# State's read in two runs one down sooner, values ahead of the last down, keys times values behind it

## The chip, the cores and the metric

The kernel runs on one core of a Trainium2 chip. The metric is the device time of one execution in microseconds; lower is better. A core has five engines with queues of their own: TensorE (PE in the profile, with its weight loads apart as PEld), VectorE (DVE), ScalarE (ACT), GpSimd (POOL) and SyncE (SP), which here only issues DMAs. Each engine works its queue off in order, and engines wait for one another through semaphores.

## The reference

A gated linear attention with a state per batch and head, and then an MLP whose activation is a SoLU with a layer norm:

```python
# q, k, v, alpha: batch 4, heads 8, seq 768, head_dim 48
for t in range(S):
    state = alpha[:, :, t, :, None] * state + np.einsum('bhd,bhe->bhde', k[:, :, t], v[:, :, t])
    y[:, :, t] = np.einsum('bhd,bhde->bhe', q[:, :, t], state)

x = y.transpose(0, 2, 1, 3).reshape(B * S, H * D)      # 3072 tokens x 384
h = x @ w_in                                           # 384 -> 1024
e = np.exp(h - h_max)
solu = h * (e / (np.sum(e, axis=-1, keepdims=True) + 1e-09))
ln = (solu - mu) / np.sqrt(var + 1e-06) * g_ln
return ln @ w_out                                      # 1024 -> 384
```

Everything is float32.

## The kernel before

**Tiles.** The sequence is cut into six groups of 128 tokens; a group holds these tokens for all four batches, 512 columns. Inside a group the attention is a masked product (scores of keys and queries, both scaled by products of alpha, times the values), and what came before the group enters through the state, which is read once per group and then renewed. The MLP of a group runs in eight steps s (0 to 7), one for each 128 of the 1024 hidden features.

**The pieces that the change and the prediction name:**

- `up(g, s)` (L382 to L407): three matmuls (w_in times x, each shown as two records) make the 512 columns of h for one step; ACT takes the exponential e (L404), DVE forms u = h*e (L405), ACT squares it (L406). h has two PSUM banks, so an up waits until the product of the up two before it has been made.
- `running` (L409): the sums of e (on POOL) and of u squared (on DVE) over the steps, into p (L421). `token_sums` (L448) turns p into sums per token by small matmuls ("rows", L456).
- `down(n, half)` (L495): for one batch of a group, eight matmuls of 385 columns against w_out, in two halves of four (L501). A group's downs are done during the next group, one half behind each up. `finish(n)` (L506): four short DVE instructions, a power on POOL (r, L532), the scaling on ACT (o_sb, L534), and the store.
- `alpha_T`, `scan_back`, `scan_on` (L187, L206, L211): transposes and scans on DVE that make the decay products. `alpha_over` (L192): two passes on ACT over the alphas as loaded, which look for values out of range; the next load of alpha may only start behind them, since it overwrites `an`.
- `keys_T`, `keys` (L222, L226): key transposes on DVE and their products with the decay on POOL.
- `scores(g, half)` (L274): 64 small matmuls (32 rows by 128) into four PSUM banks a0 to a3. `masked(half)` (L288): four DVE products that empty these banks into sT (L291).
- `read_state(half)` (L344): 32 small matmuls of q with the state into four PSUM banks y0 to y3, the same four banks as a0 to a3. `read_values` (L352): 64 small matmuls of sT with the values onto the same sums, and then four ACT copies (L359) that put them into x, the input of the next group's up.
- `next_state(g)` (L361): 64 small matmuls of keys times values, "kv", into banks a0 and a1 (so they need two of the x copies), and two additions into the state on DVE (L377). The load of v for the next group (`load_v`, L173) overwrites what kv reads.

Each of these matmuls has two records for the product and two for its weight load.

**Order.** The schedule is written by hand: the program order in Python is each engine's order. Groups 0 and 1's attention and group 0's MLP are a prologue written out (up to L811). From then on a loop runs over the groups' MLP (g = 1 to 5) and their eight steps; the attention of group g+1 is woven in by two tables, `first` for g = 1 and `usual` for the later ones. Each step does, in this order: what the table's `head` names, the up, a `finish` if one is due, at step 0 the token sums of the group before, `behind`, `running`, `middle`, one half down, `tail`. There are no downs in g = 1, since group 0's are all done in the prologue.

```python
    usual = dict(
        head={4: "keys_back", 5: "masked0", 6: "masked1"},
        behind={0: "v keys", 1: "on2 on0 on1", 2: "lasts firsts", 3: "apart", 5: "decay", 6: "alpha", 7: "back"},
        tail={4: "scores0", 5: "scores1", 6: "begin read0", 7: "values"},
        middle={7: "read1"},
    )
```

So PE's order around the end of a usual group is: up 6, half down, read0, up 7, read1, half down, values, kv, up 0 of the next group, rows.

Of the kernel before, what the change touches and what calls it, by code (L numbers as in the profile page):

```python
# [32 lines left out]
def fast_path(ctx, tc, q, k, v, alpha, moe_w_in, moe_w_out, moe_g_ln, out):  # L33
# [23 lines left out]
    HF = FC // 2  # L57
# [37 lines left out]
    over = const.tile([P, G, 2], FP, name="over")  # L95
# [35 lines left out]
    def load(src, dst, g):  # L131
        t = slice(g * P, (g + 1) * P)
        for b in range(B):
            nc.sync.dma_start(
                out=dst[32 * b : 32 * b + 32].rearrange("t h u d -> t h (u d)"),
                in_=src[b, :, t, :].rearrange("h (t u) d -> t h (u d)", u=TQ),
            )
# [40 lines left out]
    def firsts(src, dst):  # L178
        nc.vector.transpose(out=dst.rearrange("p h (t u) -> p h u t", u=TQ), in_=src[:, :, :, 0:E0])  # L179

    def lasts(src, dst):
        nc.vector.transpose(
            out=dst.rearrange("p j (i t u) -> p u j i t", u=TQ, i=2),
            in_=src[:, :, :, E0:D].rearrange("p (j i) u d -> p u j i d", i=2),
        )

    def alpha_T(g):  # L187
        nc.gpsimd.memset(aT[:, :, 0:1], 0.0)
        firsts(an, aT[:, 0:H, 1:SW])
        lasts(an, aT[:, H:NB, 1:SW])  # L190

    def alpha_over(g):  # L192
        x = an.rearrange("p h u d -> p (h u d)")
        sq = one.tile([P, 768], FP, name="sq").bitcast(U8)[:, 0 : x.shape[1]]
        for i, sign in enumerate((1.0, -1.0)):
            nc.scalar.activation(  # L196
                out=sq, in_=x, func=AF.Relu, scale=sign, bias=mone, accum_out=over[:, g, i : i + 1]
            )
# [12 lines left out]
    def scan_on(g, i):  # L211
        part = slice(NP * i, NP * i + NP)
        s = seed[i % 2]
        if i == 2:
            nc.vector.tensor_copy(out=fend[:, g], in_=h4[:, :, 1])

        least = small.tile([P, NP, 1], FP, name="least")
        nc.vector.tensor_scalar(out=least, in0=h4[:, part, 1:2], scalar1=LEAST, scalar2=None, op0=ALU.max)  # L218
        nc.vector.reciprocal(out=s[:, :, 0:1], in_=least)
        scan(aT[:, part], aT[:, part], s, False)  # L220
# [50 lines left out]
    def banks(name, shape, n=B):  # L271
        return [ps_a.tile([P] + shape, FP, tag=f"a{b}", name=f"{name}{b}") for b in range(n)]
# [71 lines left out]
    def read_state(half):  # L344
        for four in range(8 * half, 8 * half + 8, 4):
            for c in range(2):
                for n, h, e in parts[four : four + 4]:
                    for i in range(2):
                        p = slice(64 * i, 64 * i + 64)
                        y_mm(2 * i + c, n, 64 * i, state[p, c, e(h)], q64[p, c, h, 0:P])  # L350

    def read_values(g, batches=range(B)):  # L352
        if 0 in batches:
            gr[g]["x"] = pair.tile([P, KC, B, P], FP, name="x")
        for b in batches:
            for m, (n, h, e) in enumerate(parts):
                y_mm(b, n, 0, vn[:, b, e(h)], sT[:, b, h], m >= len(parts) - 4)
        for b in batches:
            nc.scalar.copy(out=gr[g]["x"][:, :, b], in_=reading["y"][b])  # L359

    def next_state(g):  # L361
        kv = banks("kv", [H, D], 2)
        for h in range(H):
            for c in range(2):
                for r in range(4):
                    b = 2 * (r // 2) + c
                    nc.tensor.matmul(
                        kv[c][quarter(r), h], lhsT=kg[:, b, h, E0 * (r % 2) : E0 * (r % 2) + E0],
                        rhs=vn[:, b, HW * h + E1 : HW * h + HW], start=True, stop=True,
                        tile_position=(0, 32 * r), skip_group_check=True,  # L370
                    )
        for c in range(2):
            s = held(state, c)
            if g == 0:
                nc.scalar.copy(out=s, in_=kv[c])
            else:
                nc.vector.tensor_tensor(out=s, in0=s, in1=kv[c], op=ALU.add)  # L377
# [114 lines left out]
        d["r"] = small.tile([P, B], FP, name="r4")  # L492
        nc.gpsimd.tensor_tensor(out=d["r"], in0=s[:, :, 3], in1=mhalf.to_broadcast([P, B]), op=ALU.pow)

    def down(n, half):  # L495
        g, b = divmod(n, B)
        d = st[n]
        if half == 0:
            d["o"] = ps_o.tile([P, 512], FP, tag="o", name="o")
        for f in range(half * HF, half * HF + HF):  # L500
            nc.tensor.matmul(  # L501
                d["o"][:, 0 : DM + 1], lhsT=u_of(g, f)[:, b * P : b * P + P], rhs=w_out[:, f], start=(f == 0),
                stop=(f == FC - 1), skip_group_check=True,
            )
# [178 lines left out]
    for i in range(3):  # L683
        part = slice(NP * i, NP * i + NP)
# [4 lines left out]
    for i in (2, 0, 1):  # L689
        if i == 1:  # L690
            scan_on(0, i)
        part = slice(NP * i, NP * i + NP)
# [66 lines left out]
    for i in range(3):  # L759
        scan_back(1, i)  # L760
        part = slice(NP * i, NP * i + NP)
# [18 lines left out]
    for i in range(2):  # L780
        scan_on(1, i)
        part = slice(NP * i, NP * i + NP)
# [12 lines left out]
    down(3, 0)  # L795
    read_begin()
    read_state(0)
    down(3, 1)
    read_state(1)
    alpha_over(2)  # L800
    load(alpha, an, 3)
    for i in range(3):
        scan_back(2, i)
    keys_T(2)
    keys(2)
    load(k, kn, 3)
    scan_on(2, 2)
    scan_on(2, 0)
    read_values(1)
    next_state(1)  # L810
    finish(3)  # L811

    usual = dict(
        head={4: "keys_back", 5: "masked0", 6: "masked1"},
        behind={0: "v keys", 1: "on2 on0 on1", 2: "lasts firsts", 3: "apart", 5: "decay", 6: "alpha", 7: "back"},
        tail={4: "scores0", 5: "scores1", 6: "begin read0", 7: "values"},
        middle={7: "read1"},
    )  # L820
    first = dict(
        head={3: "keys_back", 5: "masked0", 6: "masked1"},
        behind={0: "v", 1: "on1", 2: "lasts firsts", 3: "apart", 5: "decay", 7: "alpha back"},
        tail={4: "scores0", 5: "scores1", 6: "begin read0", 7: "values"},
        middle={7: "read1"},
    )

    def attend(a, what):

        more = a + 1 < G  # L830
        if what == "v":
            load_v(a)
        elif what == "keys":
            keys_T(a)
            keys(a)
            if more:
                load(k, kn, a + 1)
        elif what[:2] == "on":
            scan_on(a, int(what[2]))
        elif what == "lasts":  # L840
            lasts(qn, qe[:, :, 0:P])
            ends_of_decay()
            queries(2)
            move_lasts()
        elif what == "firsts":
            firsts(qn, qv[:, 0:H, 0:P])
            queries(0)
            queries(1)
            move_firsts()
            if more:  # L850
                load(q, qn, a + 1)
        elif what == "apart":
            apart()
        elif what == "decay":
            decay(a)
        elif what == "keys_back":
            if more:
                keys_back(a)
        elif what[:6] == "scores":
            scores(a, int(what[6]))  # L860
        elif what[:6] == "masked":
            masked(int(what[6]))
        elif what == "alpha" and more:
            alpha_T(a + 1)
            alpha_over(a + 1)
            if a + 2 < G:
                load(alpha, an, a + 2)
        elif what == "back" and more:
            for i in range(3):
                scan_back(a + 1, i)  # L870
        elif what == "begin":
            read_begin()
        elif what[:4] == "read":
            read_state(int(what[4]))
        elif what == "values":
            read_values(a)
            if more:
                next_state(a)

    centres = {4: (0, 1), 6: (2, 3), 7: (4, 5, 6, 7)}  # L880
    todo = []
    for g in range(1, G + 1):
        rise, att = g < G, g + 1 < G
        plan = first if g == 1 else usual

        def at(where, s):
            for what in plan[where].get(s, "").split() if att else ():
                attend(g + 1, what)

        after = None  # L890
        if not rise:
            break
        for s in range(FC):
            at("head", s)
            if rise:
                up(g, s)
            if after is not None:
                finish(after)
                after = None
            if s == 0 and g > 1:  # L900
                token_sums(g - 1)
            at("behind", s)
            for f in centres.get(s, ()) if g == 1 else ():
                centre(f)
            if rise and s:
                running(g, s)
            at("middle", s)
            if todo:
                n, half = todo.pop(0)
                down(n, half)  # L910
                if half:
                    after = n
            at("tail", s)
        if after is not None:
            finish(after)
        todo = [(n, half) for n in range(g * B, g * B + B) for half in range(2)]
# [493 lines left out]
```

## Time and profile before

| | us |
|---|---|
| median of 3 runs | 387.33 (387.31 to 387.72) |
| the profiled execution, whole | 388.88 |
| its span, first to last instruction | 387.1 |
| DVE's mask products `sT<-a,mask` (L291), mean of one | 0.683 |
| ACT's x copies `x<-y` (L359), mean of one | 0.480 |
| kv matmuls (L367), median of one record | 0.206 |

The profile shows one execution. Times in its lists are microseconds from the span's start. A line of the timeline gives start, length, engine, source line, operation, what it writes and reads, the shapes, how many instructions were merged into the line, and in brackets how long the engine was idle before it and what ended that. "issue" there means that the trace shows nothing that the engine waited for. A line of the waits gives the waiting instruction, the one that released it, the total, how many times, and the longest. Matmuls overlap in their pipeline, so what a run of them costs is read from the start of one run to the start of the next rather than from the lengths.

### The profile page before, as it was taken

The page shows a single profiled execution, that of the slowest core. Times are in us where ns is not written, and L with a number is a line of the kernel's source. Part 1 is how long each engine was busy: PE and PEld are TensorE (multiplying, and loading weights), DVE is VectorE, ACT ScalarE, POOL GpSimd, SP SyncE. Part 2 cuts the span into 40 slices and gives each one's busy share as a digit, 9 for nine tenths or more (in the row PEclk, how much of TensorE's full clock was granted, in tenths as well). Part 3 has the DMA queues.
Part 4 walks back from the last instruction along what each step waited for, and adds up shares of the span by engine and source line. Part 5 has one row for each costly group of instructions (what it writes and reads, how often), then busy time and mean ns, then how long its engine had stood idle before and what let it go on. Part 6 is the DMA issues. An engine that isn't in the chain of part 4 may idle for free. (4 is left out here: it accounts for less than half of the span.)

```text
span 387.1 us, 10060 instructions
## 1 busy us (share of the span) xinstructions
PE 365.6 (94%) x4341; PEld 219.3 (57%) x4341; DVE 250.7 (65%) x413; ACT 144.5 (37%) x255; POOL 111.5 (29%) x122
## 2 busy tenths in 40 slices
PE   8798899988979998999999999998999999999994
PEld 8685335656645556555557555665556565555652
DVE  0989878996997858885584875664875413444600
ACT  2628566681415426134253153342142132222100
POOL 6000000000232992437130466210475211323200
PEclk9989999999989999999999999999999999999999
DMA  9891978248355535717142627003123000000011
GB/s 182 166 323 51 221 220 200 47 97 183 92 131 104 116 79 102 147 35 161 37 105 47 140 62 172 13 11 70 36 63 89 22 16 8 23 21 20 22 44 47
DMA packets 72439, 36.05 MB, mean 93 GB/s; under 512 B 48185, under 2 KB 69953, under 8 KB 72385
## 3 DMA queue, kind: packets, MB, share of 16 engines
q1 hardware_dynamic: 71360, 34.39, 37.6%
q10 hardware_dynamic: 1024, 0.92, 0.7%
q8 instruction: 36, 0.59, 0.7%
q14 instruction: 19, 0.15, 0.1%
HBM read 25.30 MB, written 4.72 MB: 78 GB/s over the span
## 5 line engine op out<-in xcount | busy, mean ns | idle before, releaser
L390 PE MATMUL h<-x,w_in 128*128 128x512 f32 x288 | 134.8, 608 | 3.4 <-DVE room L405 1.6
L501 PE MATMUL o<-w_out,room 128*128 128x385 f32 x384 | 133.1, 491 | 1.1 <-DVE least L218 1.1
L501 PEld LDWEIGHTS o<-w_out,room 128*128 128x128 f32 x384 | 71.6, 190 | 56.8 <-issue 15.3
L390 PEld LDWEIGHTS h<-x,w_in 128*128 128x128 f32 x288 | 53.1, 192 | 63.5 <-issue 49.2
L405 DVE TENSOR_TENSOR room<-h,e 128x512 f32<-128x512 f32 x40 | 27.7, 693 | 62.6 <-ACT e L404 62.6
L404 ACT ACTIVATE e<-h 128x512 f32<-128x512 f32 x40 | 23.9, 597 | 89.1 <-PE h L390 88.5
L421 POOL TENSOR_TENSOR p<-p,e 128x512 f32<-128x512 f32 x30 | 40.8, 1360 | 21.9 <-ACT e L404 21.5
L406 ACT ACTIVATE u<-room 128x512 f32<-128x512 f32 x40 | 25.2, 630 | 42.5 <-DVE room L405 42.5
L532 POOL TENSOR_TENSOR r<-sums,mhalf 128x1 f32<-128x1 f32 x20 | 12.5, 626 | 91.5 <-DVE sums L524 91.5
L291 DVE TENSOR_TENSOR sT<-a,mask 128x512 f32<-128x512 f32 x44 | 27.3, 683 | 15.3 <-PE a L280 15.3
L280 PE MATMUL a<-qv,kT 32*128 32x128 f32 x704 | 26.2, 289 | 3.9 <-DVE least L218 2.0
L280 PEld LDWEIGHTS a<-qv,kT 32*128 32x128 f32 x704 | 23.2, 196 | 11.0 <-issue 2.3
L421 DVE TENSOR_TENSOR p<-p,u 128x512 f32<-128x512 f32 x30 | 23.6, 786 | 8.4 <-ACT u L406 8.4
L204 DVE TENSOR_TENSOR_SCAN hT<-aT,unit 128x516 f32<-128x516 f32 x18 | 22.3, 1285 | 8.7 <-ACT aT L677 8.6
L204 DVE TENSOR_TENSOR_SCAN aT<-aT,seed 128x516 f32<-128x516 f32 x18 | 25.0, 1391 | 0.6
L329 PE MATMUL y<-sT,vn 128*32 128x128 f32 x768 | 22.6, 273 | 0.4 <-DVE sT L291 0.4
L329 PEld LDWEIGHTS y<-sT,vn 128*32 128x32 f32 x768 | 20.7, 110 | 2.9 <-issue 2.0
L228 POOL TENSOR_TENSOR kT<-kT,hT 128x1024 f32<-128x1024 f32 (+1 forms) x8 | 13.3, 1682 | 29.8 <-DVE kT L179 29.8
L359 ACT COPY x<-y 128x384 f32<-128x384 f32 x24 | 11.2, 480 | 22.7 <-PE y L329 22.7
L196 ACT ACTIVATE sq<-an,mone 128x1536 uint8<-128x1536 f32 x12 | 18.9, 1572 | 0.2
L243 POOL COPY qe<-hT 128x4 f32<-128x4 f32 x5 | 1.0, 191 | 59.4 <-DVE hT L204 59.4
L534 ACT ACTIVATE o_sb<-o,r 128x384 f32<-128x384 f32 x16 | 9.3, 581 | 17.2 <-POOL r L532 17.2
(142 smaller groups left out, 370.2 us busy)
## 6 DMA issues: line engine op xcount, KB each, us to landing
vn<-in_v_dram SPq DMA_DIRECT2D x24, 192.0 KB, 4.5
an<-in_alpha_dram SPq DMA_DIRECT2D x20, 192.0 KB, 4.1
out_dram<-o_sb SPq DMA_DIRECT2D x20, 192.0 KB, 2.0
room<-in_moe_w_in_dram SPq DMA_DIRECT2D x6, 512.0 KB, 7.5
room<-in_moe_w_out_dram SPq DMA_DIRECT2D x8, 384.0 KB, 4.3
kn<-in_k_dram SPq DMA_DIRECT2D x16, 192.0 KB, 3.9
qn<-in_q_dram SPq DMA_DIRECT2D x16, 192.0 KB, 4.7
lot<-qe SPq DMA_DIRECT2D x40, 64.5 KB, 2.1
```

Source lines behind the costliest of these rows:

```text
L196: nc.scalar.activation(out=sq, in_=x, func=AF.Relu, scale=sign, bias=mone, accum_out=over[:, g, i : i + 1])
L204: nc.vector.tensor_tensor_scan(out=o, data0=a, data1=s, initial=1.0, op0=ALU.mult, op1=ALU.add)
L228: nc.gpsimd.tensor_tensor(out=kT[:, part], in0=kT[:, part], in1=hk[:, part], op=ALU.mult)
L280: nc.tensor.matmul(a[b][:, i], lhsT=kT[quarter(b), kb], rhs=qv[quarter(b), qb, 0:P], start=kb == h, stop=kb != h, tile_position=(32 * b, 0 ...
L291: nc.vector.tensor_tensor(out=sT[:, b, half * NP : half * NP + NP], in0=a[b], in1=mask[:, None, :].to_broadcast([P, NP, P]), op=ALU.mult,)
L329: nc.tensor.matmul(y_bank(b)[quarter(r), a], lhsT=lhsT, rhs=rhs, start=(b, r) not in begun, stop=stop, tile_position=(row, 32 * r), skip_g ...
L390: nc.tensor.matmul(h, lhsT=w_in[:, a, f * P : (f + 1) * P], rhs=d["x"][:, a].rearrange("p b t -> p (b t)"), start=(a == 0), stop=(a == KC ...
L404: nc.scalar.activation(out=e, in_=h, func=AF.Exp)
L405: nc.vector.tensor_tensor(out=u, in0=h, in1=e, op=ALU.mult)
L406: nc.scalar.activation(out=u2, in_=u, func=AF.Square)
L421: eng.tensor_tensor(out=p, in0=d[0][i] if f == 1 else p, in1=d[f][i], op=ALU.add)
L501: nc.tensor.matmul(d["o"][:, 0 : DM + 1], lhsT=u_of(g, f)[:, b * P : b * P + P], rhs=w_out[:, f], start=(f == 0), stop=(f == FC - 1), skip ...
```

## The change

In the table for the usual groups the first half of the state's read moves from behind the down of step 6 to ahead of it, the second from ahead of the down of step 7 to behind that of step 6; the values move ahead of the down of step 7, and kv stays behind it, now as an item of its own. In the table for g = 1 the values stand in the middle of step 7, ahead of `alpha_over`, and kv moves behind the first up of the next group. In the prologue, the second half of down(3) is split in two, one part ahead of the read's second half, one behind the values; the values go ahead of `alpha_over`, `finish(3)` ahead of two scans, and kv behind the first up of the loop.

```diff
-    def down(n, half):
+    def down(n, half, part=range(HF)):
         g, b = divmod(n, B)
         d = st[n]
-        if half == 0:
+        if half == 0 and 0 in part:
             d["o"] = ps_o.tile([P, 512], FP, tag="o", name="o")
-        for f in range(half * HF, half * HF + HF):
+        for f in (half * HF + i for i in part):
...
     read_state(0)
-    down(3, 1)
+    down(3, 1, (0, 1))
     read_state(1)
+    read_values(1)
     alpha_over(2)
     load(alpha, an, 3)
     for i in range(3):
...
     keys_T(2)
     keys(2)
     load(k, kn, 3)
+    down(3, 1, (2, 3))
+    finish(3)
     scan_on(2, 2)
     scan_on(2, 0)
-    read_values(1)
-    next_state(1)
-    finish(3)
...
     usual = dict(
         head={4: "keys_back", 5: "masked0", 6: "masked1"},
         behind={0: "v keys", 1: "on2 on0 on1", 2: "lasts firsts", 3: "apart", 5: "decay", 6: "alpha", 7: "back"},
-        tail={4: "scores0", 5: "scores1", 6: "begin read0", 7: "values"},
-        middle={7: "read1"},
+        middle={6: "begin read0", 7: "values"},
+        tail={4: "scores0", 5: "scores1", 6: "read1", 7: "kv"},
     )
     first = dict(
...
-        tail={4: "scores0", 5: "scores1", 6: "begin read0", 7: "values"},
-        middle={7: "read1"},
+        middle={7: "read1 values over"},
+        tail={4: "scores0", 5: "scores1", 6: "begin read0"},
     )
...
         elif what == "alpha" and more:
             alpha_T(a + 1)
+            if a > 2:
+                attend(a, "over")
+        elif what == "over" and more:
             alpha_over(a + 1)
...
         elif what == "values":
             read_values(a)
-            if more:
-                next_state(a)
+        elif what == "kv" and more:
+            next_state(a)
...
             if after is not None:
                 finish(after)
                 after = None
+            if s == 0 and g < 3:
+                next_state(g)
             if s == 0 and g > 1:
                 token_sums(g - 1)
```

## The prediction

> **What bounds the kernel now.** I read the page's busy shares first, then TensorE's (PE's) own waits, then the timeline of PE around the places that the change moves, then the clock there, last VectorE (DVE) and ScalarE (ACT) in the same stretches.
>
> ```profile
> span 387.1 us, 10060 instructions
> PE 365.6 (94%) x4341; PEld 219.3 (57%) x4341; DVE 250.7 (65%) x413; ACT 144.5 (37%) x255; POOL 111.5 (29%) x122
> ...
> PE kv L367 <- issue: 3.7, 2, 2.5
> ...
> PE kv L367 <- ACT x L359: 1.0, 1, 1.0
> PE h L390 <- ACT x L359: 0.6, 1, 0.6
> ```
> PE is the bound: 94% busy. Of its few waits, these three lines (5.3 us of idle time) all lie where the change works: at keys times values (kv) and at the up projection (h) behind the read.
>
> ```profile
> 104.18 3.70 PE L329 MATMUL y<-sT,vn 128*32 128x128 f32 x128
> 107.70 1.46 PE L367 MATMUL kv<-vn,kg 128*32 128x48 f32 x120
> 111.65 0.29 PE L367 MATMUL kv<-vn,kg 128*32 128x48 f32 x8 [2.49 <-issue]
> 111.87 9.69 PE L390 MATMUL h<-x,w_in 128*128 128x512 f32 x18
> ...
> 144.82 3.70 PE L329 MATMUL y<-sT,vn 128*32 128x128 f32 x128
> 149.57 1.86 PE L367 MATMUL kv<-vn,kg 128*32 128x48 f32 x128 [1.04 <-ACT x L359]
> 151.36 2.84 PE L390 MATMUL h<-x,w_in 128*128 128x512 f32 x6
> ...
> 201.96 3.70 PE L329 MATMUL y<-sT,vn 128*32 128x128 f32 x128
> 205.47 1.54 PE L367 MATMUL kv<-vn,kg 128*32 128x48 f32 x128
> ...
> 263.84 0.36 PE L367 MATMUL kv<-vn,kg 128*32 128x48 f32 x10 [1.23 <-issue]
> ...
> 317.71 2.84 PE L390 MATMUL h<-x,w_in 128*128 128x512 f32 x6 [0.60 <-ACT x L359]
> ```
> Five joints between two groups. The first and the fourth stop inside kv for no partner that the profile knows ("issue"), the second waits for ACT's copies of x, the third runs through, the fifth has no kv and waits for x.
>
> ```profile
> 112.32:115.74 3.42, 3.42 (x5) 1.35 (x4) 3.28 (x10) 0.00 (x0) 0.00 (x0) 0.50 0.51 126
> ...
> 113.17 1.23 DVE L204 TENSOR_TENSOR_SCAN aT<-aT,seed 128x516 f32<-128x516 f32 x1
> 114.32 0.99 DVE L377 TENSOR_TENSOR state<-state,kv 128x384 f32<-128x384 f32 x2
> ...
> 117.56 0.69 DVE L405 TENSOR_TENSOR room<-h,e 128x512 f32<-128x512 f32 x1 [1.26 <-ACT e L404]
> ```
> The windows view's last columns are granted clock, DMA share, GB/s: after the stop of 2.49 us PE had half its clock for 3.42 us. And DVE's first up product starts at 117.56 only; up(1,2), the third up projection, needs the bank that it frees (its weights load at 118.39).
>
> [...] DMA queue 8 carries 36 packets of 16,384 bytes, and counted over PE's records the two "issue" stops stand at records 3265 and 7105, 3840 = 15 x 256 apart. [...] the fetch records before the stops begin at 108.79 and 261.63 and end 1.50 and 1.28 us before PE goes on. From entering one block to running the next took 4.26 us at the first stop (DMA share 0.77 at its start) and 3.01 us at the fourth joint; 256 kv instructions alone run in 1.48 us. So a block nearly all kv starves PE. [...] (a 1.23 us scan took 1.88 beside POOL's kT products).
>
> **The change part by part.**
>
> Prices from PE's start-to-start times in group 2: up 2.57 and down 2.59 between full-array work, read half 1.09, values 3.51, kv 1.48; each border between full-array and small-tile matmuls adds 0.10 (up 2.77 and down 2.79 with small work at both sides). From the start of values to an up that only waits for x: 317.71 - 313.41 = 4.30.
>
> *Prologue.* The second half of down(3) is split around read1 and values; the x copies go ahead of alpha_over on ACT (3.5 us there), finish(3) ahead of two scans on DVE, kv behind up(1,0). PE: read0 from 99.02 to 100.30; two downs 1.5; read1 to 102.9; values to 106.4; two downs 1.4 to 107.9; x is ready at 102.9 + 4.3 = 107.2, so up(1,0) needs no wait; to 110.7; kv to 112.2; up(1,1) to 114.9. Kv now shares its block with four matmuls of down and a whole up: 0.1 + 1.4 + 2.8 + 1.3 = 5.6 us against 4.26, so the stop of 2.49 goes and with it the half clock. One block becomes tighter, that from read0 to late in read1, 3.8 us: its successor landed at 101.72, usable at some 103.1 against 102.8. Up to 0.4 us, inside the slack that follows.
>
> What is late next is DVE. It ends the key transposes at 109.31 as before, then runs finish(3) (before 115.23 to 116.30, 1.07 us). POOL's key products hold until 111.77, and the first scan could not end before 112.87 anyway; finish fits in that shadow if it isn't itself locked out (scans end at 114.4 as now), otherwise all shifts by at most 1.07. I take half, 114.9. Then comes the first up product at once: its exp is ready (POOL's r behind the key products to 112.35, o_sb 113.0, exp 113.6), where it started at 117.56 before, because state adds and finish stood ahead of it. So up(1,2) gains 2.65 us: bounds 2.15 (all locked) and 3.5 (PE's own 114.9 against 118.4). The state adds, 0.99, fit in the 1.40 us that DVE idles between two up products. Group 1 passes this on whole: its scores wait for the DVE-POOL-ACT chain, which starts with that product. **-2.65.**
>
> *Group 1 to 2.* alpha_over (1.58 x 2 + 0.19 x 2 = 3.5 us on ACT) no longer stands ahead of the x copies. Up starts 4.30 after values, at 149.12; up 2.77, kv 1.49: the token sums ("rows") start at 153.38 instead of 154.13. Their DVE input ends at 152.21 now, before that by the same shift. The exp of this up waits some 0.5 us for alpha_over, behind a PE with two full matmul runs ahead. **-0.75.**
>
> *Groups 2 to 4.* Read0 goes ahead of down in step 6, read1 behind it, values ahead of the last down, kv behind. Small runs are read0, read1, values, kv, rows where they were read0, read1, values+kv, rows: one more, two borders, **+0.2** in groups 2 and 3 each, none in group 4. Down (2.79) and kv hide the x copies as kv did. Group 3's stop goes: its joint took 264.12 - 257.63 = 6.49 against group 2's 4.99; after, its block holds one down and 233 kv, 4.2 us against 3.01. **-1.50.** Group 2's blocks come out at 5.8 and 4.28 us, the latter as now (4.23) without a stop. Group 4 has down between values and up: 4.30 - 3.51, **-0.8.**
>
> The new wait is read0 for the banks that masked1 frees. Group 2: scores end at 188.84, up ends at 191.5, the four mask products run 188.93 to 191.41. No slack, no loss: banks 1 and 3 are needed 0.3 us after 0 and 2, so 0 to 0.1 a group. Behind the waiting read0 stands only PE's own down, with it all of PE.
>
> *Queues.* SP and POOL keep their order. The alpha loads go out 7 and 3.5 us later (needed a group later), key loads behind them; the loads of v wait for kv, at 112.2 in the prologue and some 2 us later at group 1's end, wanted over 30 us on. The w_out centring on POOL gets a wait on the late downs, over 25 us old by then.
>
> **Sum:** -2.65 - 0.75 + 0.2 - 1.5 + 0.2 - 0.8 = -5.3 us. Profiled execution: span 387.1 to 381.8, with the 1.78 around it 388.88 to 383.6. The median of the runs lies 1.55 below the profiled execution: 387.33 - 5.3 = **382.0**.
>
> **Rivals.**
> - *PE paces the prologue.* If finish(3) hides in POOL's shadow and group 1's chain is no limit: 3.5 instead of 2.65, **381.2** or a little less. Against it: group 1's scores already wait for ACT and DVE.
> - *The prologue gives nothing*, since DVE, with the same work, sets group 1's pace and the product's head start is lost to POOL or transfers: the rest, -2.65, gives **384.7**. For it: DVE is at 7 to 9 tenths there.
> - *The fetch waits move rather than go.* Then only the x waits are gained: -0.75 - 0.8 + 0.4, **386.2**. Against: every block that holds kv gets a full-array run.
> - *Read0 waits for the masks (slower).* Place: step 6 of groups 2, 3, 4, where down covered them. Bounded by that down, 2.79 a group, 8.4 in all: **390.4**. It decides from 1.8 us a group on, i.e. if the masks take nearly double; they took 2.48 in each group, and DVE was idle 1.8 us ahead of them.
>
> **How the numbers follow.** Forecast (381.4 to 382.8) 0.55; PE paces 0.12; prologue gives nothing 0.15; fetch waits move 0.10; slower 0.06; no change 0.02. Some 0.2% (0.8 us) is what a measurement of this kernel can tell from no change: faster 0.91, same 0.03, slower 0.06. The range reaches from a little under the PE-paced case to a little over that without the prologue, 380.6 to 384.9; the moved fetch and the slower case stay outside.
>
> **What would show it.** Right: no "issue" stop inside kv at any joint; clock 1.00 from 100 us on; up(1,2) near 115.7; values followed by down without a wait for x; read0 starting within 0.1 us of up's end. Wrong: a stop of over 1 us at another record a multiple of 256 from 3265; half clock after 110 us; scores of group 1 starting as late as 129; or idle time before read0 put down to DVE's masks.

## The result, and the profile after

| | before | after |
|---|---|---|
| median | 387.52 us (387.31 to 389.16, 4 runs) | 382.58 us (382.24 to 383.32, 4 runs) |
| the profiled execution, whole | 388.88 | 382.77 |
| its span | 387.1 | 381.0 |

The ratio is 0.9863, 95% interval 0.9833 to 0.9894: 4.9 us by the medians. The spans differ by more, 6.1 us, and 1.2 us of that isn't the change's. The windows view of the two profiles at 20 us shows why; its last three columns are granted clock, DMA share and GB/s. First before, then after:

```profile
20.16:23.57 3.41, 3.41 (x75) 3.41 (x71) 2.24 (x3) 0.15 (x1) 0.12 (x1) 0.50 0.96 369
```

```profile
20.10:23.50 3.40, 3.22 (x111) 2.97 (x104) 3.37 (x6) 0.00 (x0) 0.12 (x1) 1.00 1.05 395
```

The profiled execution of before had half its TensorE clock for 3.41 us in the prologue, in code that both kernels share. Read0 (the first half of the state's read), the first instruction near the change, starts at 99.02 before and at 97.78 after, 1.24 us apart. The changed kernel was profiled a second time (in the last run of the experiments below): that time it had the half clock there itself, and its read0 started at 98.94. So all comparisons of profiles below count from read0.

PE's own waits after the change, longest first:

```profile
PE h L390 <- DVE room L405: 2.7, 4, 0.9
PE a L280 <- DVE least L218: 1.8, 1, 1.8
PE a L280 <- DVE qv L783: 1.2, 1, 1.2
PE o L501 <- DVE least L218: 1.1, 1, 1.1
...
PE h L390 <- ACT x L359: 0.6, 1, 0.6
```

The "issue" wait at kv and the waits for x at kv and in group 4 are gone. On top stands a wait of h for DVE's up product, and one wait for x is left. PE's timeline at the joints that the prediction showed:

```profile
101.89 3.80 PE L329 MATMUL y<-sT,vn 128*32 128x128 f32 x128
105.63 1.56 PE L501 MATMUL o<-w_out,room 128*128 128x385 f32 x4
107.03 2.74 PE L390 MATMUL h<-x,w_in 128*128 128x512 f32 x6
109.69 1.57 PE L367 MATMUL kv<-vn,kg 128*32 128x48 f32 x128
111.19 2.84 PE L390 MATMUL h<-x,w_in 128*128 128x512 f32 x6
114.83 2.84 PE L390 MATMUL h<-x,w_in 128*128 128x512 f32 x6 [0.80 <-DVE room L405]
...
145.48 2.84 PE L390 MATMUL h<-x,w_in 128*128 128x512 f32 x6 [0.61 <-ACT x L359]
148.25 1.57 PE L367 MATMUL kv<-vn,kg 128*32 128x48 f32 x128
...
257.19 1.57 PE L367 MATMUL kv<-vn,kg 128*32 128x48 f32 x128
```

Every kv now runs through without a bracket. The first joint has its new wait at the third up (0.80 us for DVE), the second keeps 0.61 us of wait for x ahead of the up.

The time falls into stretches, each from the start of one run of PE instructions to the start of another, so that nothing depends on modelled ends. All are differences to before, in microseconds, from the timelines: A is read0 to the key transposes of group 1 (22.37 before), B from there to the second half of the scores (12.36), C to group 1's token sums (20.38), D, E and F on to those of groups 2, 3 and 4 (55.59, 57.18, 53.59). What follows F took the same within 0.2 everywhere.

| | A | B | C | D | E | F | sum |
|---|---|---|---|---|---|---|---|
| the change | -2.63 | +0.21 | -0.83 | +0.32 | -1.26 | -0.68 | -4.87 |
| the change, profiled again | -2.84 | +0.24 | -0.83 | +0.32 | -1.26 | -0.68 | -5.05 |

So two profiles of one kernel agree within 0.21 us in A and 0.03 us elsewhere, and the sum fits the medians. Five of the profiles below have the change's prologue unaltered; they give -2.73 to -2.95 in A, so -2.63 is the least of seven.

### The profile page after: what moved, and what is told of

Its sections match the earlier page's. It is cut to its first block, busy times and chain, and to the rows that moved or that the text cites. A ratio compares the mean times of both kernels' runs of the same rounds, so it can differ in the third digit from the quotient of the medians.

```text
span 381.0 us, 10060 instructions
## 1 busy us (share of the span) xinstructions
PE 363.3 (95%) x4341; PEld 215.7 (57%) x4341; DVE 251.2 (66%) x413; ACT 144.3 (38%) x255; POOL 112.1 (29%) x122
## 5 line engine op out<-in xcount | busy, mean ns | idle before, releaser
L390 PE MATMUL h<-x,w_in 128*128 128x512 f32 x288 | 133.4, 601 | 3.9 <-DVE room L405 2.7
L280 PE MATMUL a<-qv,kT 32*128 32x128 f32 x704 | 24.9, 278 | 3.9 <-DVE least L218 1.8
L280 PEld LDWEIGHTS a<-qv,kT 32*128 32x128 f32 x704 | 22.0, 186 | 10.9 <-POOL p L421 2.2
```

What stands on the lines that cost most here:

```text
L280: nc.tensor.matmul(a[b][:, i], lhsT=kT[quarter(b), kb], rhs=qv[quarter(b), qb, 0:P], start=kb == h, stop=kb != h, tile_position=(32 * b, 0 ...
L390: nc.tensor.matmul(h, lhsT=w_in[:, a, f * P : (f + 1) * P], rhs=d["x"][:, a].rearrange("p b t -> p (b t)"), start=(a == 0), stop=(a == KC ...
```

## The experiments

### Each part alone

*The prologue's part* (tables as before, kv of the first joint behind the up):

```diff
-    down(3, 1)
+    down(3, 1, (0, 1))
     read_state(1)
+    read_values(1)
     alpha_over(2)
...
+    down(3, 1, (2, 3))
+    finish(3)
     scan_on(2, 2)
     scan_on(2, 0)
-    read_values(1)
-    next_state(1)
-    finish(3)
...
+            if s == 0 and g == 1:
+                next_state(g)
```

> Only the prologue's part of the change (down split, values ahead of the alpha check, finish ahead of two scans, kv of group 0 to 1 behind the first up); the tables stay as before. Theory (steps add up, DVE paces the prologue): the stop inside kv at the first joint and the half clock after it are gone, the third up of group 1 starts 2.3 to 2.7 us sooner, nothing else changes: -2.4 us, ratio 0.994. Rival (the 2.49 us stop and the half clock, 1.7 us, are worth their full length on PE): -4 us. Rival (parts need each other): under 1 us.

*The usual table alone*; the values of group 1 and the prologue stay:

```diff
     usual = dict(
...
-        tail={4: "scores0", 5: "scores1", 6: "begin read0", 7: "values"},
-        middle={7: "read1"},
+        middle={6: "begin read0", 7: "values"},
+        tail={4: "scores0", 5: "scores1", 6: "read1", 7: "kv"},
```

> Only the table of the usual groups changes (read halves one down sooner, values ahead of the last down, kv behind it). Theory: group 2 +0.3 us (one more small run), group 3 -1.26 (the fetch stop inside kv gone), group 4 -0.67: -1.6 us, ratio 0.996. The stop of 2.49 us in the prologue stays. Rival (fetch stops move rather than go): a new stop in groups 2 to 4, no gain beyond 0.7 us.

*The table of group 1 alone:*

```diff
     first = dict(
...
-        tail={4: "scores0", 5: "scores1", 6: "begin read0", 7: "values"},
-        middle={7: "read1"},
+        middle={7: "read1 values over"},
+        tail={4: "scores0", 5: "scores1", 6: "begin read0"},
...
+            if s == 0 and g == 2:
+                next_state(g)
```

> Only the table of group 1 changes (values ahead of the alpha check, kv behind the next up). Theory: token sums of group 1 start 0.75 to 0.85 us sooner, all else as before: -0.8 us, ratio 0.998; the stops in the prologue and in group 3 stay. Rival (the x copies are late for another reason than the alpha check): no change.

Measured, beside a before of 387.1 us:

| | median | ratio | A | B | C | D | E | F |
|---|---|---|---|---|---|---|---|---|
| prologue | 384.86 | 0.9926 (0.9900 to 0.9951) | -2.73 | +0.23 | +0.01 | +0.08 | -0.23 | +0.09 |
| usual table | 386.30 | 0.9976 (0.9962 to 0.9989) | -0.67 | +0.25 | +0.01 | +0.33 | -1.26 | -0.67 |
| group 1's table | 386.28 | 0.9969 (0.9952 to 0.9986) | -0.20 | 0.00 | -0.84 | 0.00 | -0.19 | +0.09 |

In its own stretches each part gains what the whole change gains there, and the three ratios add up to -1.3%, where the change has -1.4%. The parts don't need each other, and the rival that the first stop and the half clock count at full length, 4 us, is out: the prologue's part gives 2.5 us in A and B. Of the small shares elsewhere, the -0.67 in A for the usual table is taken up below; the -0.23 and -0.19 in E are in part a shorter stop of group 3 (1.09 and 1.13 us instead of 1.23), and 0.09 of them comes back in F. The usual table's median gains 0.8 us only, where its stretches D to F give 1.60 and 1.6 was forecast; its interval reaches to 1.5 us. Its executions ranged from 385.36 to 387.70, and what the rest is isn't shown.

That run of the usual table shows more. Its PE timeline in the prologue, where its program is that of before:

```profile
106.16 1.46 PE L367 MATMUL kv<-vn,kg 128*32 128x48 f32 x120
109.70 0.29 PE L367 MATMUL kv<-vn,kg 128*32 128x48 f32 x8 [2.08 <-issue]
109.92 5.42 PE L390 MATMUL h<-x,w_in 128*128 128x512 f32 x12
116.70 2.84 PE L390 MATMUL h<-x,w_in 128*128 128x512 f32 x6 [1.36 <-DVE room L405]
```

A stop again, 0.41 us shorter, but no half clock behind it this time: two ups take 5.42 us. Yet A and B together are only 0.42 us shorter (-0.67 and +0.25), since PE now waits 1.36 us for DVE ahead of the third up. So before, the stop and the half clock stood almost wholly behind DVE: in DVE's timeline of before, which the prediction shows, the state additions start at 114.32 right behind a scan and without a wait, 2.4 us after the end of kv (111.65 + 0.29).

### Are the stops the arrival of instructions?

The kernel before, with 72 more PE records ahead of everything:

```diff
-            nc.tensor.matmul(t[:, 0:P], lhsT=ones, rhs=ones, start=True, stop=True)
+            nc.tensor.matmul(t[:, 0:HW], lhsT=ones, rhs=ones[:, 0:HW], start=True, stop=True)
...
-    warm(18)
+    warm(36)
```

> The kernel before with 36 warm-up matmuls of 64 columns instead of 18 of 128: 18 more matmuls, 72 more PE records ahead of everything else, the same PE work in columns. Theory (stops are the arrival of instruction blocks of 256): every stop comes 72 records earlier in the program. First joint: the stop stands after some 84 of the 128 kv records instead of 120, about 2.0 us. Group 3's joint: after some 82 instead of 118, about 0.8 us. Group 2's joint, which had none, gets one after some 112 kv records, about 1.3 us, since its block now holds 31 records of values and 225 of kv. Group 1's gets none. Time about 0.4 us over before. Rival (the stops are a wait that belongs to the last kv matmuls, such as a PSUM bank or a transfer): they stay after 120 and 118, and group 2 stays free.

PE's timeline at the first joint and at group 2's:

```profile
118.52 1.10 PE L367 MATMUL kv<-vn,kg 128*32 128x48 f32 x84
121.36 0.70 PE L367 MATMUL kv<-vn,kg 128*32 128x48 f32 x44 [1.73 <-issue]
...
216.60 1.44 PE L367 MATMUL kv<-vn,kg 128*32 128x48 f32 x115
219.11 0.37 PE L367 MATMUL kv<-vn,kg 128*32 128x48 f32 x13 [1.07 <-issue]
```

The first stop moved from after 120 to after 84 matmul records, as forecast to the record, and group 2 got a stop where it had none (115 records, forecast 112). Counted over all PE records, they stand at 3265 and 5825, again 193 plus multiples of 256. What is called a block here is a stretch of 256 PE records from such a number on; that the records come in such stretches is read from the places of the stops. The page of before says what queue 8 carries:

```profile
q8 instruction: 36, 0.59, 0.7%
```

In before, one packet of this queue, 16,384 bytes each, lies in each of the three stretches ahead of the first stop: from 100.84, 104.71 and 108.79, where the stretches end at 103.83, 107.39 and 111.65. A wait that belonged to the last kv matmuls would have stayed. Group 3's stop, forecast at 0.8 us, shrank below 0.5 us.

The time doesn't show what the stops cost: 400.52 us, ratio 1.0324 (1.0294 to 1.0353). The 72 records of 64 columns ran 15.62 us where 36 of 128 columns had taken 6.88, about 0.2 us a record in both, so read0 comes 10.9 us later. The same again with a warm-up of the old length:

```diff
+        for i in range(tiny):
+            nc.tensor.matmul(t[0:1, 0:1], lhsT=ones[:, 0:1], rhs=ones[:, 0:1], start=True, stop=True)
...
-    warm(18)
+    warm(13, tiny=23)
```

> The kernel before with 13 warm-up matmuls of 128 columns and 23 of one column instead of 18 of 128: again 72 more PE records ahead, now without a longer warm-up. Theory (blocks of 256): stops where the other kernel with 72 more records had them, 1.7 us after 84 of the kv records at the first joint, 1.1 us or a little more after 112 at group 2's, under 0.5 us at group 3's. Against before: -0.4 in the prologue, +1.7 in group 2, -0.9 in group 3, so +0.4 us, with the prologue's share uncertain by the clock. Rival: the extra time of the other kernel came with the records, not with its warm-up: +10 us.

389.42 us, ratio 1.0061 (1.0039 to 1.0082). Its PE timeline at the three joints:

```profile
107.30 1.10 PE L367 MATMUL kv<-vn,kg 128*32 128x48 f32 x84
110.10 0.70 PE L367 MATMUL kv<-vn,kg 128*32 128x48 f32 x44 [1.70 <-issue]
110.74 5.42 PE L390 MATMUL h<-x,w_in 128*128 128x512 f32 x12
117.93 2.84 PE L390 MATMUL h<-x,w_in 128*128 128x512 f32 x6 [1.78 <-DVE room L405]
...
207.32 0.37 PE L367 MATMUL kv<-vn,kg 128*32 128x48 f32 x13 [0.94 <-issue]
...
263.46 0.71 PE L367 MATMUL kv<-vn,kg 128*32 128x48 f32 x46 [0.54 <-issue]
```

The stops are where the other shifted kernel had them, so 10 us weren't the records' doing. The stretches give -0.18, +0.17, 0.00, +1.27, -0.70, 0.00, together +0.56, which fits the forecast of +0.4. The median is 1.9 us over before, more than that; its executions ranged from 388.57 to 391.76, and where the rest lies the one profile doesn't show. So the forecast holds for the stretches, and not for the time.

This profile also prices the first stop. It lasts 1.70 us here instead of 2.49, no half clock follows, and PE reaches the third up early enough to wait 1.78 us for DVE; but A and B together are only 0.01 us shorter than before (0.20 in the first shifted kernel). The 0.8 us of stop and the half clock that are missing here had cost next to nothing, and a shorter stop yet would only lengthen PE's wait.

### Does DVE pace the prologue?

The changed kernel with `finish(3)` behind the two scans:

```diff
-    finish(3)
     scan_on(2, 2)
     scan_on(2, 0)
+    finish(3)
```

> The changed kernel with finish(3) back behind the two scans of the prologue. Theory (DVE paces the prologue, and the first exp waits for the scaling of finish): the scans end about 1 us sooner, finish behind them, its power and scaling follow, so the first up product comes about 1.5 us later than in the changed kernel (1.3 to 1.6 us behind the end of finish) and the third up waits that much longer: +1.2 to +1.5 us on the changed kernel. Rival (PE paces the prologue there): no difference.

383.87 us, ratio to before 0.9905 (0.9872 to 0.9938). A is -1.68 against -2.63 and -2.84 in the two profiles of the change, so 0.95 to 1.16 us are lost, a little under the forecast. PE's and DVE's timelines:

```profile
115.68 2.84 PE L390 MATMUL h<-x,w_in 128*128 128x512 f32 x6 [2.30 <-DVE room L405]
```

```profile
113.06 0.61 DVE L528 SCALAR_TENSOR_TENSOR o_mean<-mean_sb,sums,o 128x384 f32<-128x384 f32 x1
114.93 0.69 DVE L405 TENSOR_TENSOR room<-h,e 128x512 f32<-128x512 f32 x1 [1.27 <-ACT e L404]
```

PE's wait for the third up grows from 0.80 to 2.30 us: the up product now waits for its exp, which on ACT stands behind the scaling of `finish(3)`. A stays 1.68 us under before even so. In before the state additions (0.9 us, from 114.32 to 115.23) stood between the scans and the first product; here, with kv behind the first up, they follow it. No run moves them alone, so their share is read from the timelines.

The opposite edit, on the faster kernel described below: the second scan behind the first up product.

```diff
     scan_on(2, 2)
-    scan_on(2, 0)
...
     first = dict(
...
-        behind={0: "v", 1: "on1", 2: "lasts firsts", 3: "apart", 5: "decay", 7: "alpha back"},
+        behind={0: "v on0", 1: "on1", 2: "lasts firsts", 3: "apart", 5: "decay", 7: "alpha back"},
```

> The run before with the prologue's second scan moved behind the first up product and the state additions. Theory (the DVE chain, not PE, paces group 1 up to its scores): the first up product comes 1.5 us sooner and PE's wait of 0.8 us for it goes, but the scan then fills DVE's idle time and the second up product comes when it did: scores of group 1 start no more than 0.3 us sooner. Rival (PE paces): all of 0.8 us gained.

382.06 us against 381.65 without it, ranges overlapping. PE's timeline:

```profile
110.50 5.42 PE L390 MATMUL h<-x,w_in 128*128 128x512 f32 x12
115.75 1.47 PE L299 MATMUL tp<-ident,kT 128*128 128x128 f32 x12
117.06 5.32 PE L390 MATMUL h<-x,w_in 128*128 128x512 f32 x12
123.50 0.60 PE L280 MATMUL a<-qv,kT 32*128 32x128 f32 x8 [1.12 <-POOL qv L256]
124.43 2.84 PE L280 MATMUL a<-qv,kT 32*128 32x128 f32 x56 [0.33 <-ACT qv L248]
```

The wait for the third up, 1.05 us without this edit, is gone and A is 1.3 us shorter, and the scores then wait 1.12 us for POOL, where they had waited 0.29. Counted from read0 they start 0.5 us sooner (25.88 instead of 26.37), more than the 0.3 forecast and half of the wait that went. Then a stretch of half clock, from 125.41 for 3.41 us, takes more than that back (B +2.65). So the chain over DVE, POOL and ACT sets the time of group 1's scores, and a wait of PE ahead of it is worth only a part of its length.

### Where kv may stand

Two edits of the changed kernel. In the first, group 1's kv stands ahead of the next up again (the alpha check stays behind the x copies):

```diff
     first = dict(
...
-        tail={4: "scores0", 5: "scores1", 6: "begin read0"},
+        tail={4: "scores0", 5: "scores1", 6: "begin read0", 7: "kv"},
...
-            if s == 0 and g < 3:
+            if s == 0 and g == 1:
```

> The changed kernel with kv of group 1 ahead of the next up instead of behind it (the alpha check stays behind the x copies). Theory: up no longer waits 0.6 us for x, since kv's 1.48 us stands between; but the instruction block that ends inside this kv then holds 144 records of values and 112 of kv, 2.6 us of work against 3.0 or more from entry to use: a stop of 0.4 to 1.5 us inside kv after some 56 of its 128 records. Net -0.2 to +0.9 us on the changed kernel. Rival (no fetch stop): -0.6 us and no idle time inside kv.

In the second, kv of groups 2 and 3 stands behind the next up, next to the token sums:

```diff
     usual = dict(
...
-        tail={4: "scores0", 5: "scores1", 6: "read1", 7: "kv"},
+        tail={4: "scores0", 5: "scores1", 6: "read1"},
...
-            if s == 0 and g < 3:
+            if s == 0 and g < G - 1:
```

> The changed kernel with kv of groups 2 and 3 also behind the next up, next to the token sums (one run of small matmuls fewer in each). Theory: group 3 gains 0.2 to 0.3 us (two borders); group 2's block from kv's 29th record on holds 227 records of kv and 29 of token sums, 1.6 us of work, and gets a stop of some 1.4 us or more in the token sums: +0.8 us or more in all. Same edit, opposite sign in two groups. Rival (small runs cost, fetch doesn't): -0.5 us, both groups gain.

382.66 us, ratio 0.9862 (0.9830 to 0.9895), and 382.36 us, ratio 0.9851 (0.9817 to 0.9885). Here the rivals were right, and the rule that a block takes 3 us or more from PE's entry into the block ahead of it was not. Stretch C of the first is -1.51 where the change has -0.83; D and E of the second are +0.01 and -1.59 where the change has +0.32 and -1.26. The timelines, of the first and of the second:

```profile
145.57 1.54 PE L367 MATMUL kv<-vn,kg 128*32 128x48 f32 x128
147.04 2.84 PE L390 MATMUL h<-x,w_in 128*128 128x512 f32 x6
```

```profile
199.56 2.86 PE L501 MATMUL o<-w_out,room 128*128 128x385 f32 x8
202.26 2.74 PE L390 MATMUL h<-x,w_in 128*128 128x512 f32 x6
204.93 1.57 PE L367 MATMUL kv<-vn,kg 128*32 128x48 f32 x128
206.31 0.64 PE L456 MATMUL rows<-p,ones 128*32 128x64 f32 x32
```

No stop in either, although the block that ends in the second's token sums (record 5825) was run 1.41 us after the one before it (5569, entered at 205.10). The fetch records of DMA queue 8 say how: that block's fetch began at 202.34, 2.76 us ahead of PE's entry into the block before. The fetch began while PE still worked on full-array matmuls (8 records in 2.70 us from 199.56 on, where kv's 128 records take 1.38). In the first edit the fetch began only 0.26 us behind the entry (143.77 against 143.51), and the block was run 2.63 us after it, without a stop. At the stops of before the fetch began 0.8 us (group 3) and 1.4 us (prologue) behind the entry. At those that the shift brought to group 2 it was only 0.29 and 0.18 us, but there PE was through the block ahead in 1.87 us (2.94 - 1.07 and 2.81 - 0.94). What all stops inside kv share is the time from the start of the fetch to the block's first instruction, 2.2 to 2.9 us; in the second edit PE came to the block 4.17 us after it. So these stops had both: a fetch that began late, and a block ahead that PE was through in less than that.

The first edit with the 72 further records of 64 columns:

> The same as the run with kv of group 1 ahead of the up, with 72 more PE records ahead (36 warm-up matmuls of 64 columns instead of 18 of 128). Theory: the block that ended inside kv now ends 72 records earlier, its work is 216 records of values and 40 of kv, 3.2 us, so the stop of that run is gone or under 0.3 us; the read of group 1 in the prologue gets a block of 3.1 us and up to 0.8 us of stop, hidden by PE's wait for DVE: -0.3 to -0.6 us on the changed kernel. Rival (kv ahead stalls for another reason, such as the PSUM banks): the idle time stays.

392.79 us, ratio 1.0128 (1.0098 to 1.0157), for the longer warm-up; C is -1.53 as without them, so there was no stop for the shift to remove.

### Both

```diff
     usual = dict(
...
-        tail={4: "scores0", 5: "scores1", 6: "read1", 7: "kv"},
+        tail={4: "scores0", 5: "scores1", 6: "read1"},
...
     first = dict(
...
-        tail={4: "scores0", 5: "scores1", 6: "begin read0"},
+        tail={4: "scores0", 5: "scores1", 6: "begin read0", 7: "kv"},
...
-            if s == 0 and g < 3:
+            if s == 0 and g != 2 and g < G - 1:
```

> The changed kernel with kv of group 1 ahead of the next up, and kv of groups 2 and 3 behind the next up, next to the token sums. Both edits gained in the profiles of the runs before (0.68 us at the joint of groups 1 and 2, 0.31 and 0.33 at the next two), against what the 3 us rule for an instruction block said. If they add: -1.3 us on the changed kernel, no stop inside kv. If the two together make a dense run of instructions where neither alone did: a stop at a record that is 193 plus a multiple of 256.

381.65 us (380.88 to 382.56), ratio to before 0.9842 (0.9820 to 0.9863), the fastest median of all. The changed kernel beside it:

> The changed kernel again, beside these runs on the same chip: 4.5 to 5.5 us under before. Whether a half-clock stretch near 20 us is in its profile [...]; with it the span is some 1.2 us longer from there on.

383.32 us (382.26 to 383.77), ratio 0.9882 (0.9859 to 0.9904): 4.2 us under before, below the 4.5 expected. The two intervals touch, so that the version with both is faster than the change isn't settled by the times; its stretches C, D and E (-1.34, +0.03, -1.58 against -0.83, +0.32, -1.26) say 1.1 us. C lacks 0.17 us of what the first edit alone gave: kv at that joint took 1.73 us instead of 1.54, with a new block in its midst 2.61 us after that block's fetch began. That is a stop too short for the timeline's brackets, where none was forecast if the two edits add.

## Why the prediction was right

The forecast was 382.0 us, from a sum of -5.3; it came to 382.58 and -4.9, and by the profiles -4.87. By its terms:

- **Prologue, -2.65.** A and B together gave -2.42. The gain comes from where the prediction looked for it, from DVE's order: `finish(3)` ahead of the scans and the state additions behind the first up product. The stop inside kv and the half clock went as well, but in the profiles without that half clock they had been worth little. The third up's wait, now for DVE, is where the prediction put it. The term that was mis-sized is the time that DVE is held up beside POOL ("locked out" in the prediction): half of 1.07 us was taken for `finish(3)` beside POOL's key products, and all of it came. From the end of the key transposes to the end of the scans DVE took 5.10 us before and 6.26 after. DVE's timeline after:

```profile
108.00 1.35 DVE L521 SCALAR_TENSOR_TENSOR t<-sums 128x1 f32<-128x1 f32 x1
109.39 1.11 DVE L524 TENSOR_TENSOR sums<-t,s 128x1 f32<-128x1 f32 x1
...
112.97 1.23 DVE L204 TENSOR_TENSOR_SCAN aT<-aT,seed 128x516 f32<-128x516 f32 x1
114.12 0.66 DVE L405 TENSOR_TENSOR room<-h,e 128x512 f32<-128x512 f32 x1
```

  Two instructions on a single column took 1.35 and 1.11 us, where they take 0.16 elsewhere in the same kernel; POOL's two products ended at 109.34 and 110.48, each within 0.02 us of the end of one of them. The copy just ahead of them (0.14 us) wasn't held. In before a copy of 12 columns (L215) took 1.55 us, until 0.03 us behind POOL's first product, and 0.16 us in the profile after, where it stands behind both. Which instructions are held, and why, isn't shown beyond these. The first up product starts 16.34 us after read0, 18.54 before: 2.20 us sooner, near the lower of the stated bounds (2.30 to 2.51 in six other profiles with this prologue).

  That A and B still came to -2.42 is in a small part luck. The forecast set the third up's gain equal to the product's. But before, PE was late as well: its third up started at 118.82, 0.55 us behind what the product allowed (after, the up starts 0.71 us behind its product), and the second exp waited for the second up, some 0.2 us. So A gains more than the product, B gives a part of it back, and 0.2 us of PE's own lateness made good half of what the hold-up beside POOL took. One block of instructions was called tighter, at up to 0.4 us, inside the slack; that fits the first up, which starts 9.25 us after read0 here and 8.71 or 8.72 in three other profiles with this prologue; PE's wait ahead of the third up took it in (0.80 us against 1.03 to 1.05).
- **Group 1 to 2, -0.75:** -0.83, and -0.84 alone.
- **Group 2, +0.2:** +0.32. The borders were the mis-sized term: values ahead of a down take 3.63 us to the down's start (194.85 to 198.48), where 3.51 was taken from values ahead of kv. That is 0.12 us more with a change from small to full-array matmuls behind the values; no run prices a border alone.
- **Group 3, -1.5 + 0.2:** -1.26, the stop gone.
- **Group 4, -0.8:** -0.68, by the same border: 4.30 - 3.63 (305.38 to 309.01).
- **The new wait of read0 for the masks:** none. PE's timeline in group 2 shows no bracket at read0:

```profile
184.33 2.84 PE L390 MATMUL h<-x,w_in 128*128 128x512 f32 x6
187.11 1.17 PE L329 MATMUL y<-lot,state 64*32 64x128 f32 x64
```

- **The profiled execution's distance to the median,** 1.55 us, was carried over as a constant. It was for the most part the half clock at 20 us (1.24 us by the starts of read0), which that execution had. The carrying over was right for the median; the profile after happened to lack the half clock, which is why the span moved by 6.1 us and the median by 4.9.

Of the rivals, PE pacing the prologue fell with the two experiments on DVE, the prologue that gives nothing with the prologue alone, and the moved fetch stops with the profile after. The rule behind the fetch argument, so many microseconds from entry to use, held for the places of the stops and not for its cases without one: it counted from PE's entry, where what the stops share is the 2.2 to 2.9 us from the start of the fetch. It did no harm in the forecast, since every block of the change that holds kv has a full-array run in it.

## What to carry to other kernels

Here long runs of small matmuls used up instructions faster than they arrived: 256 of kv ran in 1.48 us, and at the stops a block's first instruction came 2.2 to 2.9 us after its fetch began. What told it was an "issue" stop that kept to record numbers of 193 plus a multiple of 256 when 72 records were added ahead. In the change a few full-array matmuls between two such runs removed it. Work that PE could do anyway is best put where PE would wait for copies, between the read and the matmuls that need it. Before a wait of the bound engine is priced at its length, look which chain is next: group 3's stop of 1.23 us was worth about its length, the prologue's 2.5 us of stop and 3.4 us of half clock hardly anything, for DVE stood right behind, and what gained some 2.2 of the 2.4 us there was DVE's own order. No run takes the prologue's stop away and leaves DVE's order as it was; this rests on the three profiles in which the stop was 0.4 to 0.8 us shorter and the half clock missing, for 0.0 to 0.4 us in A and B.

## What the runs showed of the hardware

- An execution may or may not have 3.4 us of half clock early on: before had it (from 20.16 on, behind a PE wait of 2.04 us); the changed kernel had it in one profile (from 20.10 on, behind a PE wait of 1.94 us) and not in the other (behind one of 1.77 us), and read0 came 1.2 us apart. The wait of 2.49 us in the prologue was followed by it, and so was one of 2.25 us in the run of group 1's table; one of 2.08 us and one of 2.30 us were not. The length of a wait alone doesn't tell, and what starts a half clock isn't shown; that the stop brought it in the prologue was the author's estimate.
- Stops at a block of instructions weren't bound to kv, and differed between profiles: the run with both edits had no half clock at 20 us, but a stop of 1.59 us at 26.73, inside the values of group 0, at record 961 (193 plus 3 x 256), and its read0 came at 98.81, as late as with the half clock. At the same record the changed kernel's profile has 0.48 us (25.67).
- Float32 matmuls on a full weight tile cost about 0.2 us a record early in the program whether they have 64 or 128 columns (15.62 us for 72, 6.88 us for 36), so a warm-up of narrower matmuls isn't shorter per instruction.
